# A ring of three load slots whose length becomes a multiple of 256 bytes

## The chip, the cores and the metric

The kernel runs on one core of a Trainium2 chip. A core has five engines with queues of their own: TensorE (PE in the profile, with its weight loads as PEld), VectorE (DVE), ScalarE (ACT), GpSimd (POOL) and SyncE (SP). Data comes from the memory outside the core through 16 DMA engines into the on-chip memory SBUF, which has 128 partitions; a tile here has a row of so many bytes in each partition. Matrix products are written into a second on-chip memory, PSUM.

The metric is the device time of one execution in microseconds (us), and the median over several executions is compared.

## The reference

Two attention blocks decode one token against a cache of 8192 positions, and a gate mixes their outputs. Everything is float32.

```python
# x: 1x1x448.  A: 16 heads with 16 key/value heads.  B: 16 heads with 8 key/value heads.  Dh = 256
q = (x @ wq).reshape(16, 256)
scores = q @ k_cache.T * 256 ** -0.5          # per head, 8192 positions
p = softmax(scores)
o = p @ v_cache                                # per head, 256
out = o.reshape(16 * 256) @ wo                 # 448
g = sigmoid((x * gate_w).sum())
result = g * out_A + (1 - g) * out_B           # both from the same x
```

The two caches make nearly all of the input: 24 key/value heads of 8192 x 256 numbers, for keys and for values, are 403 MB; with the projection matrices the core reads 432 MB, each byte once.

## The kernel before

**One stream.** The host lays all inputs end to end in one array, `stream`, in the order in which the kernel wants them. The function `plan()` makes that order. It goes over eight sets; a set is one key/value head of B (with two query heads) and two heads of A. Each head's keys and values are cut into four tiles of 128 partitions x 4096 numbers (`ROWS * DH`), and a value tile follows its key tile three tiles later (`LEAD`). Query weights (`wq`) come ahead of the set that they serve, output weights (`wo`) behind it.

**Fills.** `plan()` cuts the stream into 54 fills, `LOADS`, without regard to where a tile ends: a fill has 15872 numbers (`FULL`) for each partition, 63488 bytes, and the first has 8 numbers (`XG`) more, the input vector and the gate weights. Fills 0 to 50 are loaded by one DMA each. The last three are cut into smaller DMAs, 2, 3 and 7 of them. So 50 loads move 128 rows of 63488 bytes, and load 0 moves 128 rows of 63520 bytes. In the stream the rows of a load lie end to end.

**The ring.** Line 464 takes a buffer `buf`, named `slot`, from the pool `ring`, which has `SLOTS = 3` buffers and uses them in turn. The length of a buffer is `FULL + XG` = 15880 numbers, 63520 bytes of a partition, since the first fill needs that much. Line 468 issues the load on SyncE's queue, into the buffer from its first byte on (`c` is 0 at the start of each fill). SyncE waits there until the engines have read what the buffer held three fills before; this is what sets the order of loads against compute. The engines then wait for the load's semaphore.

The pools follow one another in a partition: `const` up to byte 8960, the ring from there, and the pool of working tiles, `small`, behind it. In the built program the three slots begin at bytes 8960, 72480 and 136000. Loads 0, 3, 6, ... go to 8960 (called slot A here), loads 1, 4, 7, ... to 136000 (slot C), and loads 2, 5, 8, ... to 72480 (slot B). The number 8960 is 35 x 256; 72480 is 32 past a multiple of 256, and 136000 is 64 past one.

**What the engines do with a slot.** `piece()` takes each part of a fill to its consumer. Keys of most heads are laid out transposed, and `scores()` multiplies them with the query on TensorE (line 255); VectorE takes the minimum of the negated scores (line 261), ScalarE the exponential (264), and VectorE transposes the result (267). For the first head of A in each set (`BY_ROW`), `scores_by_row()` does the product on VectorE: line 277 multiplies the key tile with the query in place, in the slot, and line 281 sums each position's 256 products. `attend()` multiplies the weights with the value tile on TensorE (line 307). Every fourth tile, a head is closed: `take`, `gather`, `combine`, `column` and `project_o` turn its sums into 256 numbers, and `emit_set` multiplies a set's heads with `wo` (line 380). The last set's output weights arrive last, and `emit` (line 397), a copy (line 482) and the store (line 483) end the program.

Of the kernel before, what the change touches and what calls it, by code (L numbers as in the profile page):

```python
# [7 lines left out]
F32 = mybir.dt.float32  # L8
# [6 lines left out]
P = 128  # L15
# [12 lines left out]
FULL = 15872  # L28
# [12 lines left out]


XG = 2 * (KF + 1)
ATOM = {"xg": XG, "k": 2 * DH, "v": 2 * DH, "wq": 2 * DH, "wo": D}


def plan():

    size = {"xg": XG, "k": ROWS * DH, "v": ROWS * DH, "wq": WQ, "wo": 8 * D}
    per = len(UNITS) * NT  # L50
# [15 lines left out]
    for kind, i in items[:items.index(last[0])]:  # L66
        at, left = 0, size[kind]
        while left:
            step = min(left, room) // ATOM[kind] * ATOM[kind]
            if step:  # L70
# [24 lines left out]
def kernel(  # L95
# [9 lines left out]
    ring = ctx.enter_context(tc.tile_pool(name="ring", bufs=SLOTS))  # L105
# [309 lines left out]
    def piece(kind, i, at, view):  # L415
        n = view.shape[-1] // ATOM[kind]
        j0 = at // ATOM[kind]
        if kind == "xg":
            inputs(view[:, :KF + 1])
            GW[0] = view[:, KF + 1:]  # L420
        elif kind == "wq":
            project(i, j0, view.rearrange("p (c n) -> p c n", c=n))
            if j0 + n < 2 * KF + 1:
                pass
            elif i == 0:
                spread(0)
                prepare(GW[0])
            else:
                wait(1, spread, i)
        elif kind == "k":  # L430
            u, t = TILES[i]
            if u in BY_ROW:
                scores_by_row(u, t, 2 * j0, view.rearrange("p (j d) -> p j d", d=DH))
            else:
                scores(u, t, j0, view.rearrange("p (c n) -> p c n", c=n))
            if j0 + n < 2 * NG:
                return
            tick()
            if t == NT - 1:
                gather(u)  # L440
                wait(1, combine, u)
                wait(2, column, u)
        elif kind == "v":
            u, t = TILES[i]
            n = view.shape[-1] // DH
            attend(u, t, at // DH, n, view.rearrange("p (j d) -> p j d", d=DH))
            if at // DH + n == ROWS:
                if t == NT - 1:
                    take(u)
                    if u != TILES[-1][0]:  # L450
                        wait(1, project_o, u)
                if i >= len(TILES) - LEAD:
                    tick()
        elif kind == "wo" and i < NS - 1:
            emit_set(i, j0, view.rearrange("p (c n) -> p c n", c=n))
            if i == NS - 2 and j0 + n == 8:
                fold()
        else:
            for j in range(n):
                LAST[divmod(j0 + j, 2)] = view[:, j * D:(j + 1) * D]  # L460

    off = 0
    for fill in LOADS:
        buf = ring.tile([P, FULL + XG], F32, name="slot")
        c = 0
        for load in fill:
            n = sum(x[3] for x in load)
            nc.sync.dma_start(buf[:, c:c + n], stream[off:off + P * n].rearrange("(p n) -> p n", p=P))
            off += P * n
            for x in load:  # L470
                piece(*x[:3], buf[:, c:c + x[3]])
                c += x[3]
# [78 lines left out]
```

## Time and profile before

| | us |
|---|---|
| median of 3 runs | 1010.08 |
| lowest and highest run | 1009.97, 1012.16 |
| span of the profiled execution, first to last instruction | 1008.4 |

The profiled execution's own time is known by its span alone; the rest of the 1010.08 us lies around the span, or is the difference of that execution to the median.

How to read the lines below. The page's first part gives for each engine its busy time, its share of the span and the number of its instructions. The second part cuts the span into 40 slices and gives busy tenths, for the DMA engines too. The third gives for a DMA queue the packets, the megabytes and the time of these packets as a share of 16 engines' time; asked for a stretch of time, the same view counts the packets that start in it, with their whole time, so in a short stretch the share can be over 100%. The fourth is the chain of work that ended last, followed back from the end; in its long form each row has a start, a length and a name, and a DMA's length goes from the issue to the landing. DMA issues are listed with their size and the time from issue to landing. In rows of waits stand the total, the number and the longest. `L281` is line 281 of the kernel.

### The profile page before, as it was taken

How to read it: one execution, taken by the hardware profiler on the slowest of the kernel's cores; microseconds unless marked ns; L12 is line 12 of the kernel's file. 1: busy time of each engine (PE TensorE's matmuls, PEld its weight loads, DVE VectorE, ACT ScalarE, POOL GpSimd, SP SyncE). 2: the span in 40 equal slices, each digit the busy share in tenths (PEclk: the TensorE clock that was granted, in tenths of full speed). 3: DMA queues.
4: the chain of work that ended last, by engine and by line, in shares of the span. 5: the costliest groups of instructions: out<-in, count | busy, mean ns of one | idle time of the engine just before them, and what ended most of it. 6: DMA issues, size and time to landing. Idle time of an engine off the chain costs nothing.

```text
span 1008.4 us, 7568 instructions
## 1 busy us (share of the span) xinstructions
PE 584.2 (58%) x3154; PEld 171.4 (17%) x3154; DVE 458.2 (45%) x644; ACT 92.8 (9%) x307; POOL 1.9 (0%) x10
## 2 busy tenths in 40 slices
PE   0855845664655555746646576655665637536567
PEld 0211211121111111212111121111211112111112
DVE  1386213961248521576214841248521585206851
ACT  0100100010100110001100000100110100101010
POOL 0000000000000000000000000000000000000000
PEclk9877787777787787877777767776787867877878
DMA  9999999999999999999999999999999999999997
GB/s 403 442 438 418 434 436 439 418 441 431 441 436 426 424 441 438 429 426 442 431 428 441 431 429 434 436 434 431 432 431 441 439 423 424 439 443 431 418 426 310
DMA packets 9113, 432.49 MB, mean 429 GB/s; under 512 B 1016, under 2 KB 1144, under 8 KB 1784
## 3 DMA queue, kind: packets, MB, share of 16 engines
q1 hardware_dynamic: 9080, 432.02, 99.2%
q8 instruction: 24, 0.39, 0.2%
q14 instruction: 9, 0.07, 0.0%
HBM read 432.02 MB, written 0.00 MB: 428 GB/s over the span
## 4 chain that ended last, share of the span: by engine, by line
DMA 72%; DVE 15%; PE 11%; ACT 1%; issue 1%; another core or an unknown queue 0%; SPq 0%; ACTq 0%; DVEq 0%
DMA slot<-in_stream_dram 72%; DVE sr L281 6%; DVE slot L277 6%; PE o L307 5%; PE sc L255 4%; PE sm L220 1%; ACT px L264 0%; DVE mn L261 0%; DVE pr L294 0%; ACT pxr L290 0%; DVE pr L267 0%; ACT ew L346 0%; DVE wr L353 0%; PE sm L371 0%; DVE mt L287 0%
## 5 line engine op out<-in xcount | busy, mean ns | idle before, releaser
L307 PE MATMUL o<-slot,pr 128*32 128x512 f32 (+1 forms) x1536 | 352.4, 764 | 220.2 <-DMA slot<-in_stream_dram 220.2
L255 PE MATMUL sc<-slot,qb 128*32 128x512 f32 x1024 | 199.0, 725 | 102.5 <-DMA slot<-in_stream_dram 102.3
L261 DVE TENSOR_REDUCE mn<-sc 128x1 f32<-128x512 f32 x64 | 44.1, 690 | 334.3 <-PE sc L255 311.5
L277 DVE TENSOR_TENSOR slot<-slot,qa 128x4096 f32<-128x4096 f32 (+7 forms) x40 | 142.6, 3565 | 43.6 <-DMA slot<-in_stream_dram 43.6
L307 PEld LDWEIGHTS o<-slot,pr 128*32 128x32 f32 (+1 forms) x1536 | 80.6, 143 | 403.5 <-DMA slot<-in_stream_dram 249.0
L281 DVE TENSOR_REDUCE sr<-slot 128x16 f32<-128x4096 f32 (+7 forms) x40 | 142.7, 3567 | 1.4
L255 PEld LDWEIGHTS sc<-slot,qb 128*32 128x32 f32 x1024 | 47.1, 132 | 221.2 <-issue 125.5
L264 ACT ACTIVATE px<-sc,st 128x512 f32<-128x512 f32 x64 | 44.0, 687 | 408.1 <-DVE st L262 366.5
L267 DVE STREAM_TRANSPOSE pr<-px 128x512 f32<-128x512 f32 x64 | 45.6, 713 | 59.5 <-ACT px L264 59.5
L220 PE MATMUL sm<-slot,xz 128*32 128x512 f32 x128 | 47.2, 717 | 36.8 <-DVE xz L193 22.9
L290 ACT ACTIVATE pxr<-sr,st 128x16 f32<-128x16 f32 x32 | 9.8, 308 | 372.9 <-DVE st L288 372.9
L371 PE MATMUL sm<-sel,ob 128*128 128x1 f32 (+1 forms) x96 | 18.2, 294 | 36.6 <-DVE ob L317 36.6
L317 DVE SCALAR_TENSOR_TENSOR ob<-o,half,ob 128x256 f32<-128x256 f32 x24 | 11.3, 473 | 43.6 <-ACT ob L316 43.6
L371 PEld LDWEIGHTS sm<-sel,ob 128*128 128x128 f32 x96 | 16.2, 237 | 60.5 <-DVE ob L317 54.9
L220 PEld LDWEIGHTS sm<-slot,xz 128*32 128x32 f32 x128 | 11.3, 129 | 67.0 <-issue 28.4
L294 DVE TENSOR_TENSOR pr<-pxr,cols 128x256 f32<-128x256 f32 x32 | 13.6, 426 | 15.9 <-ACT pxr L290 15.9
L237 PE MATMUL sm<-px,spread 64*128 64x256 f32 x16 | 7.1, 533 | 14.4 <-DVE es L347 14.4
L360 PE MATMUL sm<-ones,wr 1*128 1x1 f32 x48 | 9.6, 268 | 9.2 <-DVE wr L353 9.2
L316 ACT ACTIVATE ob<-o,half 128x256 f32<-128x256 f32 x24 | 11.3, 469 | 39.7 <-PE o L307 39.6
L380 PE MATMUL Y<-slot,ocs 128*1 128x448 f32 x112 | 14.1, 621 | 0.0
L360 PEld LDWEIGHTS sm<-ones,wr 1*128 1x128 f32 x48 | 7.8, 203 | 32.6 <-issue 32.6
L264 ACT ACTIVATION_READ_ACCUMULATOR px<-sc,st 128x1 f32 x64 | 12.3, 193 | 0.0
(73 smaller groups left out, 137.5 us busy)
## 6 DMA issues: line engine op xcount, KB each, us to landing
slot<-in_stream_dram SPq DMA_DIRECT2D x50, 7936.0 KB, 42.5
slot<-in_stream_dram SPq DMA_DIRECT2D x1, 7940.0 KB, 21.8
slot<-in_stream_dram SPq DMA_DIRECT2D x1, 4864.0 KB, 41.2
slot<-in_stream_dram SPq DMA_DIRECT2D x2, 2048.0 KB, 25.3
slot<-in_stream_dram SPq DMA_DIRECT2D x1, 3072.0 KB, 30.1
slot<-in_stream_dram SPq DMA_DIRECT2D x1, 1280.0 KB, 20.8
slot<-in_stream_dram SPq DMA_DIRECT2D x1, 1024.0 KB, 23.5
slot<-in_stream_dram SPq DMA_DIRECT2D x2, 512.0 KB, 24.8
```

Source lines behind the costliest of these rows:

```text
L220: nc.tensor.matmul(q[BLK * a:BLK * (a + 1), :], xz[:, c if c < KF else KF + a, :], w[:, j, :], start=(c == 0), stop=(c == KF), skip_group_ ...
L255: nc.tensor.matmul(sc[32 * g:32 * (g + 1), :], qb[:, e, at:at + 32], kt[:, j, :], start=(e == 0), stop=(e == 1), skip_group_check=True)
L261: nc.vector.tensor_reduce(mn, sc, axis=AX.X, op=OP.min)
L264: nc.scalar.activation(px, sc, AF.Exp, bias=st[:, 0, t:t + 1], scale=-1.0, accum_out=st[:, 1, t:t + 1])
L267: nc.vector.transpose(pr.rearrange("p (q r k) -> p q k r", r=BLK, k=2), px.rearrange("p (q k c) -> p q k c", c=BLK, k=2))
L277: nc.vector.tensor_tensor(kt, kt, QA[u][:, None, :].to_broadcast([P, n, DH]), op=OP.mult)
L281: nc.vector.tensor_reduce(sc[:, j0:j0 + n], kt, axis=AX.X, op=OP.add)
L294: nc.vector.tensor_tensor(pr, px[:, :, None, :].to_broadcast([P, ROWS // 2, NG * NT, 2]), cols[:, t].rearrange("p g r -> p (g r)")[:, None ...
L307: nc.tensor.matmul(O[u][w * g:w * (g + 1), :], pr[:, j // 2, :w], vt[:, j - j0:j - j0 + 2, :], start=(t == 0 and j < 2 * P // w), stop=(t ...
L360: nc.tensor.matmul(cl, WR.pop(u).rearrange("p c x m k -> p (c x m k)"), ones[:1, :], start=True, stop=True)
L371: nc.tensor.matmul(oc[:, e, :M], OB[u][:, e::2], SEL[u][:, :M], start=True, stop=True)
L380: nc.tensor.matmul(YY[0][32 * h:32 * h + 1, :], OC[s, r][:, e, m:m + 1], wt[:, j, :], start=False, stop=(s == NS - 2 and e == 1), skip_gro ...
```

## The change

A slot becomes 15936 numbers long in place of 15880, which is 63744 bytes of a partition, 249 x 256, in place of 63520. The three slots then begin at bytes 8960, 72704 and 136448, all multiples of 256, and the working tiles behind the ring begin at byte 200192 in place of 199520. What is loaded, in which order and into which slot in turn, stays; so do the sources in `stream`. The last 56 numbers of a slot are never written or read.

```diff
 XG = 2 * (KF + 1)
+SLOT = 15936
 ATOM = {"xg": XG, "k": 2 * DH, "v": 2 * DH, "wq": 2 * DH, "wo": D}
...
     for fill in LOADS:
-        buf = ring.tile([P, FULL + XG], F32, name="slot")
+        buf = ring.tile([P, SLOT], F32, name="slot")
         c = 0
```

## The prediction

> **What bounds the kernel now.** I read the page's first three parts, then the chain that ended last, then the DMA issues, and last the DMA view of single microseconds. The page first:
>
> ```profile
> span 1008.4 us, 7568 instructions
> PE 584.2 (58%) x3154; PEld 171.4 (17%) x3154; DVE 458.2 (45%) x644; ACT 92.8 (9%) x307; POOL 1.9 (0%) x10
> ...
> DMA  9999999999999999999999999999999999999997
> ...
> q1 hardware_dynamic: 9080, 432.02, 99.2%
> ...
> DMA 72%; DVE 15%; PE 11%; ACT 1%; issue 1%; another core or an unknown queue 0%; SPq 0%; ACTq 0%; DVEq 0%
> ```
>
> No engine is busy for 60% of the span, while the 16 DMA engines are busy in every slice and at 99.2% in all. The chain gives DVE 15% and PE 11%, and a reader could take those for work that the transfers wait for. They are not. The chain follows SyncE's issue of a load back to the engine that freed the slot, but when that issue comes the earlier loads are still streaming. Two rows of the DMA issues show it, the first load (issued at 0.74 us with nothing ahead of it), and the load issued at 214.24 us, the shortest landing that the view gives for any later full load:
>
> ```profile
> slot<-in_stream_dram SPq DMA_DIRECT2D x1, 7940.0 KB, 21.8
> slot<-in_stream_dram SPq DMA_DIRECT2D x1, 7936.0 KB, 34.7
> ```
>
> A load with free engines lands 21.8 us after its issue; the most hurried later one takes 34.7, so it stood 12.9 us in line. The transfers never ran dry: a slot could be freed up to 12.9 us later and no byte would be later. The bound is the pace of the transfers, and the chain in order of time tells it (start, length; start plus length is a landing):
>
> ```profile
> 81.06 36.75 DMA slot<-in_stream_dram
> ...
> 127.38 46.64 DMA slot<-in_stream_dram
> ...
> 192.92 37.30 DMA slot<-in_stream_dram
> ...
> 545.30 42.38 DMA slot<-in_stream_dram
> ...
> 607.34 36.54 DMA slot<-in_stream_dram
> ...
> 985.78 18.75 DMA slot<-in_stream_dram
> ...
> 1004.57 0.99 PE Y L397 x32
> ```
>
> Landings at 117.81, 174.02 and 230.22 us lie 56.21 and 56.20 apart, those at 587.68 and 643.88 again 56.20: each time three loads, one into each slot, so 18.73 us a load of 7936 KB, or 434 GB/s. The last landing is at 1004.53, and 3.9 us of tail follow. The span is 1008.4 and the median of the runs 1010.08, so 1.7 us lie around the span or between that execution and the median; I keep them.
>
> **The change part by part.** It has two effects. The first is where a load's rows begin. Slot A, for loads 0, 3, 6 and so on, begins at byte 8960 of a partition before and after, 35 times 256. Slot C, for loads 1, 4, 7, moves from 136000 (64 bytes past a multiple of 256) to 136448 (a multiple). Slot B, for loads 2, 5, 8, moves from 72480 (32 bytes past) to 72704. So the kernel before already holds the experiment: a third of its loads are aligned. What a misaligned row costs is the difference between the slots' row transfers. The DMA view over windows of 1.00 us that hold nothing but whole rows of 63488 bytes gives it; the last number is the time of these rows as a share of 16 engines' time in the window. First slot A (load 45, from 852.53 us), then C (load 46, from 871.24), then B (load 47, from 889.93):
>
> ```profile
> q1 hardware_dynamic: 15, 0.95, 219.6%
> ...
> q1 hardware_dynamic: 15, 0.95, 219.6%
> ...
> q1 hardware_dynamic: 15, 0.95, 220.1%
> ```
>
> 219.6% of 16 us over 15 rows is 2342.4 ns a row in slots A and C; 220.1% is 2347.7 ns in slot B. Being 64 bytes past costs nothing that shows; being 32 past costs 5.3 ns. Slot B earlier, load 5 from 100.38 us and load 20 from 383.38 us:
>
> ```profile
> q1 hardware_dynamic: 15, 0.95, 219.7%
> ...
> q1 hardware_dynamic: 14, 0.89, 205.4%
> ```
>
> These are 2343.5 and 2347.4 ns. So the extra is about 1 ns early and 5 ns from somewhere before load 20 on. A load is 128 rows, 8 for each of 16 engines (8 x 2342.4 ns is 18.74 us, the chain's 18.73). Slot B takes 17 whole loads (2, 5, ... 50). If all paid 5.3 ns, the change is worth 17 x 8 x 5.3 ns = 0.72 us. If loads 20 to 50 pay 5.3 and the six before pay 1.1, it is 8 x (11 x 5.3 + 6 x 1.1) ns = 0.52 us. The chain speaks for less: with 5.3 ns on one load of three, a late cycle should be 0.04 us longer than an early one, and 643.88 - 587.68 is 56.20, as early. The extra may lie within engines that aren't the last to land, and then it is worth nothing. The ends are 0.72 us and 0; I take 0.4, near their middle, since one kind of row supports each end. Slot C adds 0: its row reads as A's. Could an aligned row cost more than a misaligned one? The windows exclude it, since A's rows are nowhere above B's or C's.
>
> The Trainium skill, page "DMA: Bandwidth & Descriptors", section "How a descriptor splits into AXI transactions", says that a transfer that doesn't begin on a 256-byte boundary starts its first transaction at the boundary below and pays the skipped bytes in beats of 32 bytes. By it slot B would lose one beat a row and slot C two; at 1.18 ns a beat (2342.4 ns for 1984 of them) 17 x 8 x 3 x 1.18 ns makes 0.48 us, an estimate from that page, and the time would be 1009.6 us. The trace agrees in size and disagrees in which slot: C, with two beats to lose, loses none.
>
> The second effect is a shift of everything behind the ring. The working tiles (`px`, `pr`, `st` and the rest) begin at 200192 in place of 199520, and SyncE, TensorE, VectorE, ScalarE and GpSimd get the same instructions with the same waits in the same order; no DMA is added, split or moved past another. Engine operands in slots B and C shift too. No row shows the working tiles at another address, so I bound their cost by the slots, which three addresses do show. VectorE's two passes over a k tile:
>
> ```profile
> L281 DVE TENSOR_REDUCE sr<-slot x40: 686/4420/4422, 52.2 to 960.5; 128x16 f32<-128x4096 f32 x24, 128x4 f32<-128x1024 f32 x3, 128x12 f32<-128x3072 f32 x3, 128x10 f32<-128x2560 f32 x2
> ...
> L277 DVE TENSOR_TENSOR slot<-slot,qa 128x4096 f32<-128x4096 f32 x24 | 106.0, 4418 | 18.7 <-DMA slot<-in_stream_dram 18.7
> ```
>
> The full reduction has median 4420 and maximum 4422 ns over tiles in all three slots, so an offset of 32 or 64 bytes moves it by 2 ns or less. I cost the shift at zero. What hides it otherwise is the 12.9 us in line. In the tail it isn't covered: 3.9 us of small work after the last landing, of which even 5% would be 0.2 us, up or down.
>
> Sum, on the profiled span: 1008.4 - 0.4 + 0 = 1008.0, and on the median 1010.08 - 0.4 = 1009.7 us, which is 0.04% and less than a measurement of this kernel can tell from no change (about 0.2%, 2.0 us; its three runs went from 1009.97 to 1012.16).
>
> **The rivals.** *The change touches the transfers not at all.* The 5.3 ns may belong to the third place in the cycle and its neighbours in time, not to the address. Load 5's 1.1 ns at the same address and C's zero speak for it; that the extra is there in windows of loads 20 and 47 speaks against. Time 1010.1 us. The Trainium skill's page "SBUF — State Buffer", section "A bandwidth-pool intuition that's wrong (but worth ruling out)", would also have it so: HBM, at about 358 GB/s a core, is nearly always what limits, not SBUF. Here the rate is 434, so this run doesn't sit at that figure.
>
> *Faster by more than 0.2%.* Misalignment costs at each 256-byte piece of a row, not only at its head, so that both other slots gain. A row has 248 such pieces, and its 2342.4 ns come to 1.18 ns for 32 bytes; if each piece lost the time of 32 bytes, that would be 293 ns a row, 34 x 8 x 293 ns = 80 us in all, and 930 us. To reach 2.0 us, 7.4 ns a row in both slots are enough (34 x 8 x 7.4 ns). C's 0 and B's 5.3 say no; only a cost between rows, outside their recorded time, could hide it.
>
> *Slower by more than 0.2%.* With all three slots equal modulo 256, VectorE's passes over one slot and the writes into another begin at like offsets and get in each other's way. The place is the release of a slot by L281:
>
> ```profile
> SPq L468 <- DVE sr L281: 477.3, 24, 24.2
> ```
>
> A slot holds at most 3.9 tiles of 4096 and so at most 3.9 x (4418 + 4420) ns = 34.5 us of the two passes. The point of decision is 12.9 us more than that, 37%; at 50% a release would be 17.2 us later, 4.3 beyond the cover, and once in each of the eight sets that is 34 us, 1044. Against it: slot A and slot C sit 64 bytes apart already, and no pass in the span exceeds the median by more than 2 ns.
>
> **How the numbers follow.** The small gain (1009.7) gets 0.52, no effect (1010.1) 0.38, the faster rival 0.04, the slower one 0.03, and 0.03 goes to a median that lands 0.2% high by the spread of runs alone, as one of the three runs shown did. The first two are both within 0.2%: same 0.90, faster 0.04, slower 0.06. The range takes 0.72 us of gain and a further 0.7 for the runs below (1008.6), and above reaches into the spread of the runs shown, 1011.2, short of the highest.
>
> **What would show it.** Right: windows in loads of slot B read 219.6% for 15 rows, late in the span as well; cycles of three loads stay at 56.20 us; the DMA share stays at 99%; L281 keeps 4420 ns. The first rival shows if B keeps its 220.1% at its new address. The prediction is wrong if a cycle falls below 56.1 us, which only a cost between rows explains, or if a full load lands in about 22 us, which means that the line ran dry.

## The result and the profile after

| | before | changed |
|---|---|---|
| median | 1010.32 us (21 runs) | 1008.87 us (21 runs) |
| lowest, highest | 1009.83, 1012.16 | 1008.40, 1010.60 |
| ratio of the changed kernel to the one before | | 0.9986 (95% interval 0.9980 to 0.9991) |

The changed kernel is 1.45 us faster, with an interval of 0.9 to 2.0 us. That is 0.14%, in the forecast range and within the 0.2% that was called no change, but about three and a half times the 0.4 us that was forecast. The span varies less than the whole time: its median is 1008.2 us over the 93 runs of the kernel before that stood beside the experiments (1008.1, 1008.3 and 1008.2 in their three groups), and 1007.0 over the 21 runs of the changed one. So some 1.2 us of the 1.45 lie inside the span.

The page of the changed kernel has the same shape: span, engines, the DMA line and the first queue.

```profile
span 1007.7 us, 7568 instructions
PE 570.9 (57%) x3154; PEld 167.4 (17%) x3154; DVE 458.1 (45%) x644; ACT 92.7 (9%) x307; POOL 1.9 (0%) x10
...
DMA  9999999999999999999999999999999999999997
...
q1 hardware_dynamic: 9080, 432.02, 99.2%
```

The DMA share is 99.2% as before: the transfers are still the bound, and only their pace can have changed. The DMA view over a window of 1.00 us that holds nothing but rows of 63488 bytes, in load 45 (slot A, from 851.84 us), load 46 (C, from 870.56) and load 47 (B, from 888.62):

```profile
q1 hardware_dynamic: 11, 0.70, 161.0%
...
q1 hardware_dynamic: 11, 0.70, 161.0%
...
q1 hardware_dynamic: 10, 0.63, 146.4%
```

161.0% of 16 us over 11 rows and 146.4% over 10 are 2341.8 and 2342.4 ns, which is the same within the rounding of the share. Slot B's 2347.7 ns are gone; all three slots read alike. The chain in order of time shows what it did to the pace:

```profile
193.10 37.20 DMA slot<-in_stream_dram
...
237.92 48.51 DMA slot<-in_stream_dram
...
545.49 41.83 DMA slot<-in_stream_dram
...
604.25 39.21 DMA slot<-in_stream_dram
...
653.56 46.00 DMA slot<-in_stream_dram
...
984.88 18.49 DMA slot<-in_stream_dram
1003.41 1.45 PE Y L398 x32
```

Landings at 230.30 and 286.43 lie 56.13 us apart, those at 587.32, 643.46 and 699.56 lie 56.14 and 56.10 apart, where the kernel before had 56.20. These cycles of three loads are 0.06 to 0.10 us shorter. They are single ones; by the mean start of a load's 128 rows in the packet records, a cycle became 0.07 us shorter from load 17 to load 50 and 0.03 us from load 2 to load 17. The last landing came at 1003.37 in place of 1004.53, 1.16 us earlier. The spans of these two executions differ by 0.7 us only, since what follows the last landing took 4.3 us in place of 3.9. VectorE's sum over a tile is what it was, at a median of 4420 ns:

```profile
L282 DVE TENSOR_REDUCE sr<-slot x40: 686/4420/4421, 52.1 to 959.7; 128x16 f32<-128x4096 f32 x24, 128x4 f32<-128x1024 f32 x3, 128x12 f32<-128x3072 f32 x3, 128x10 f32<-128x2560 f32 x2
```

### The profile page after: what moved, and what is told of

It reads as the page before. It is cut to its first block, busy times and chain, and to the rows that moved or that the text cites. A ratio compares the mean times of both kernels' runs of the same rounds, so it can differ in the third digit from the quotient of the medians.

```text
span 1007.7 us, 7568 instructions
## 1 busy us (share of the span) xinstructions
PE 570.9 (57%) x3154; PEld 167.4 (17%) x3154; DVE 458.1 (45%) x644; ACT 92.7 (9%) x307; POOL 1.9 (0%) x10
## 3 DMA queue, kind: packets, MB, share of 16 engines
q1 hardware_dynamic: 9080, 432.02, 99.2%
## 4 chain that ended last, share of the span: by engine, by line
DMA 72%; DVE 15%; PE 11%; ACT 1%; issue 1%; another core or an unknown queue 0%; SPq 0%; ACTq 0%; DVEq 0%
DMA slot<-in_stream_dram 72%; DVE sr L282 6%; DVE slot L278 6%; PE o L308 5%; PE sc L256 4%; PE sm L221 1%; ACT px L265 0%; DVE mn L262 0%; DVE pr L295 0%; ACT pxr L291 0%; DVE pr L268 0%; ACT ew L347 0%; DVE wr L354 0%; PE sm L372 0%; DVE mt L288 0%
## 5 line engine op out<-in xcount | busy, mean ns | idle before, releaser
L308 PE MATMUL o<-slot,pr 128*32 128x512 f32 (+1 forms) x1536 | 342.6, 737 | 225.8 <-DMA slot<-in_stream_dram 225.8
L282 DVE TENSOR_REDUCE sr<-slot 128x16 f32<-128x4096 f32 (+7 forms) x40 | 142.7, 3567 | 1.4
## 6 DMA issues: line engine op xcount, KB each, us to landing
slot<-in_stream_dram SPq DMA_DIRECT2D x1, 7940.0 KB, 22.1
```

What stands on the lines that cost most here:

```text
L282: nc.vector.tensor_reduce(sc[:, j0:j0 + n], kt, axis=AX.X, op=OP.add)
L308: nc.tensor.matmul(O[u][w * g:w * (g + 1), :], pr[:, j // 2, :w], vt[:, j - j0:j - j0 + 2, :], start=(t == 0 and j < 2 * P // w), stop=(t ...
```

## The experiments

Each was timed in five rounds against the kernel before. The table at the end of this section gives, besides the times, the mean length of a row in each slot.

**All slots 32 past.** An unused tile ahead of the ring moves three equally spaced slots.

```diff
+    head = ctx.enter_context(tc.tile_pool(name="head", bufs=1))
     ring = ctx.enter_context(tc.tile_pool(name="ring", bufs=SLOTS))
...
+    spare = head.tile([P, 8], F32, name="spare")
+    nc.vector.memset(spare, 0.0)
...
-        buf = ring.tile([P, FULL + XG], F32, name="slot")
+        buf = ring.tile([P, 15936], F32, name="slot")
```

> Slots are 63744 bytes long as in the changed kernel, and an unused tile of 32 bytes stands ahead of the ring, so all three slots begin 32 bytes past a multiple of 256. Theory 1 (the address: a row that begins at an odd multiple of 32 bytes takes longer): every load pays what slot B paid before. Rows in windows of all three slots read about 2347 ns, and with the 1.45 us that 17 loads cost, 51 loads cost 4.3 us over the changed kernel, 1013.2 us; by 5.3 ns a row it is 2.2 us and 1011.1. Theory 2 (the third place in the cycle, with slots of unequal spacing): spacing is that of the changed kernel, so 1008.9 and rows at 2342 ns. Theory 3 (the beats skipped below a 256-byte boundary, one here): 1.18 ns a row, 0.5 us, 1009.4.

Measured: 1011.41 us, 1.0013 of the kernel before (1.0004 to 1.0022). Rows of loads 45 (slot A, from 853.43 us) and 47 (B, from 890.94):

```profile
q1 hardware_dynamic: 15, 0.95, 220.1%
...
q1 hardware_dynamic: 16, 1.02, 234.7%
```

These are 2347.7 and 2347.0 ns, in slot A too, which had been free. The time is near the 1011.1 us that the rows' price gave, and not the 1013.2 of three times the measured gain. The place in the cycle (theory 2, no cost) and the skipped beats (theory 3, 1.18 ns a row) fall. What stands is a cost of some 5.5 ns a row for an address 32 past, in any slot.

**All slots 64 past.** The same with a spare tile of 16 numbers; the lines show the difference to the kernel with 32.

```diff
-    spare = head.tile([P, 8], F32, name="spare")
+    spare = head.tile([P, 16], F32, name="spare")
```

> As the kernel before this one, with 64 unused bytes ahead of the ring: all three slots begin 64 bytes past a multiple of 256. Theory 1 (odd multiples of 32): 64 is free, rows at 2342 ns, 1008.9 us, as the changed kernel. Theory 3 (skipped beats, two here): 2.4 ns a row, rows at 2344.8 ns, 51 x 8 x 2.4 ns = 1.0 us more, 1009.9. If only multiples of 256 are free for another reason, about what the kernel with 32 bytes shows.

Measured: 1010.66 us, 1.0007 (0.9998 to 1.0015). Rows of loads 45 (from 852.81 us) and 46 (from 878.59):

```profile
q1 hardware_dynamic: 13, 0.83, 190.7%
...
q1 hardware_dynamic: 14, 0.89, 205.4%
```

2347.1 and 2347.4 ns; over the late loads, 17 to 50, the mean is 2346.6. So 64 past is not free, and theory 1, which took odd multiples of 32 alone for the cause, falls in this form. But then slot C of the kernel before, 64 past, should have paid, and in its windows it did not.

**The old ring, 32 further on.** The slots keep 63520 bytes, and the spare tile of 8 numbers stands ahead: A 32, C 96, B 64 past.

```diff
+    head = ctx.enter_context(tc.tile_pool(name="head", bufs=1))
     ring = ctx.enter_context(tc.tile_pool(name="ring", bufs=SLOTS))
...
+    spare = head.tile([P, 8], F32, name="spare")
+    nc.vector.memset(spare, 0.0)
```

> The slots keep the old length of 63520 bytes, and 32 unused bytes stand ahead of the ring: slot A begins 32, slot B 64 and slot C 96 bytes past a multiple of 256. Theory 1 (odd multiples of 32): loads of A and C pay and B, the one that paid before, doesn't; rows about 2347 ns in A and C and 2342 in B; 34 loads cost twice what 17 did, 1008.9 + 2.9 = 1011.8 us (1010.3 to 1011.8, as the rows or the medians price it). Theory 2 (third place in the cycle): B alone pays, 1010.3. Theory 3 (skipped beats 1, 2 and 3): all three pay, 2.0 x 1.18 ns a row on average, 1009.9.

Measured: 1010.71 us, 1.0006 (0.9997 to 1.0015). All three slots pay: means of 2347.4 (A, 32), 2346.4 (C, 96) and 2346.6 ns (B, 64). None of the three theories gives that: the skipped beats have all three pay, but 1.2, 3.5 and 2.4 ns, with C the dearest.

**Only the working tiles moved.** A gap of 672 bytes behind the old ring.

```diff
+    gap = ctx.enter_context(tc.tile_pool(name="gap", bufs=1))
...
+    spare = gap.tile([P, 168], F32, name="spare")
+    nc.vector.memset(spare, 0.0)
```

> The ring is that of the kernel before (slots of 63520 bytes, B 32 past a multiple of 256), and 672 unused bytes behind it put the working tiles at byte 200192, where the changed kernel has them. If the slots' address is the whole cause, 1010.3 us with B's rows at 2347 ns late in the span. If the place of the working tiles gave the part of the 1.45 us that the rows don't explain (0.7 us), 1009.6.

Measured: 1010.06 us, 1.0000 (0.9991 to 1.0008), with the row means of the kernel before to 0.1 ns. The interval reaches about 0.9 us to either side, and the median span, 1008.2 us, is that of the kernel before; so the place of the working tiles has no part in the gain that these runs can tell.

**C alone at 64.** From here on the slots are those of the changed kernel, and the load is written from a later byte of its slot. What is added to `c` counts numbers of 4 bytes. The line with `enumerate` stands in every kernel from here on except the one at 16, and isn't shown again.

```diff
-    for fill in LOADS:
+    for place, fill in enumerate(LOADS):
...
-        c = 0
+        c = (0, 16, 0)[place % 3]
```

> The slots of the changed kernel, all on multiples of 256, but loads 1, 4, 7, ... (slot C) are written from byte 64 of the slot, so C alone is 64 past, as it was in the kernel before, and A and B are aligned. In the kernel before, rows of C read 2342 ns, in the kernel with all slots at 64 they read 2346.6. If the offset itself costs (the kernel before hid it for some reason of its own), rows of C read 2346.6 and the time is 1008.9 + 17 x 8 x 4.6 ns = 1009.5 to 1009.8 us. If 64 is free in company of aligned slots and costs where its neighbours cost, rows of C read 2342 and the time is 1008.9.

Measured: 1008.80 us, 0.9986 (0.9977 to 0.9995): as fast as the changed kernel, with a third of its loads misaligned. Load 46 (slot C, from 877.23 us):

```profile
q1 hardware_dynamic: 11, 0.70, 161.0%
```

2341.8 ns, and 2342.1 over C's late loads. A misaligned load with two aligned ones ahead of it is free at 64.

**The two offsets exchanged.** C at 32, B at 64.

```diff
-        c = 0
+        c = (0, 8, 16)[place % 3]
```

> Aligned slots; loads of C are written from byte 32 and loads of B from byte 64, the two offsets of the kernel before with places exchanged. Theory of the address: C's rows read 2347.5 and B's 2346.6 or 2342; by the medians of the four runs so far 1010.0 to 1011. Theory of the place (what comes third in the cycle pays, if it isn't aligned): B's rows read 2346 to 2348, C's 2342, 1010.3. In both the sum of the rows' excess says the time: 1.4 us for each us that the mean row's excess makes in a DMA engine.

Measured: 1010.08 us, 0.9999 (0.9990 to 1.0008), the time of the kernel before. Load 46 (C, from 871.25 us) and load 47 (B, from 889.83):

```profile
q1 hardware_dynamic: 15, 0.95, 219.6%
...
q1 hardware_dynamic: 14, 0.89, 205.2%
```

2342.4 ns in C, and 2345.1 in B, with a mean of 2346.9 over B's late loads. It is again the second misaligned load of the two that pays most, and now that one is at 64. So it isn't the address alone; what came ahead counts. Within C the rows are not alike: with the 128 rows of load 25 in order of their start, sixteen at a time, the means are 2342.0, 2342.0, 2342.0, 2342.0, 2342.5, 2344.6, 2348.8 and 2347.7 ns. The last groups hold rows of the next load too, since the 16 engines aren't in step.

The records don't name the engine, but they let the rows be joined. A row starts 3 to 4 ns before the end of another one, and 2 to 3 ns after it where a new load begins; followed from end to start, the rows fall into 16 lines of work, one for an engine, with 8 rows a load. Where two engines end together a join can be mistaken. Joined so, the eight rows of an engine read, as means over the late loads, 2342.0 to 2342.3 ns in the first five of C and 2344.2, 2347.7 and 2347.8 in its last three; 2345.9 to 2347.4 in B; and in A, which is aligned, still 2345.4, 2343.7 and 2342.9 in the first three, then 2342.0. The price sets in within C and fades within A.

**All loads at 128, and at 16.** Two more offsets; the first pair of lines is the one at 128 bytes, the second the one at 16.

```diff
-        c = 0
+        c = (32, 32, 32)[place % 3]
...
-        c = 0
+        c = 4
```

> Aligned slots, every load written from byte 128 of its slot. Excess of a row so far: 5.4 ns at 32, 4.6 at 64, 4.5 at 96 (all loads unaligned). If it is a matter of 256 alone, rows at 128 cost about the same, 4.0 to 4.6 ns, and the time is 1010.5 to 1010.9. If 128 is a boundary of its own, rows read 2342 and the time is 1008.9. By skipped beats (four) it would be 4.7 ns at 128, but then 64 should have been 2.4 and 32 1.2.

> Aligned slots, every load written from byte 16 of its slot, so a row begins in the middle of a 32-byte piece, which neither kernel does. If only the head and tail of a row cost, rows read 2347 to 2350 ns and the time is 1011 to 1013. If every 32-byte piece of the row is touched twice, rows take up to twice as long and the time goes towards 2000; already one further 256-byte piece in ten (25 of 248, 9.4 ns each) would be 0.24 us a row and 1105 us.

Measured: 1010.76 us at 128, 1.0007 (0.9998 to 1.0016), and 1011.85 us at 16, 1.0018 (1.0010 to 1.0027). 128 isn't a boundary of its own. A row that begins in the middle of a 32-byte piece costs 6.6 ns, too little for a cost at each piece; it must lie at few places of the row, such as its head and tail. With all loads misaligned the prices are 6.6 ns at 16, 5.6 at 32, 4.6 at 64 and 4.3 at 128.

**Every other load at 32.**

```diff
-        c = 0
+        c = 8 * (place % 2)
```

> Aligned slots of 63744 bytes; even loads are written from byte 0 of the slot and odd loads from byte 32, so each of 25 whole misaligned loads stands between two aligned ones. So far a full load at 32 costs 2.55 us / 51 = 0.05 us (1011.4 against 1008.85). If every misaligned row pays, 25 loads cost 1.25 us: 1010.1. If a DMA engine has some 36 ns in hand that misaligned rows use up (5.4 ns each at 32) and aligned rows restore, the first six or seven of its eight rows in an odd load read 2342 ns and the rest 2347, some 8 ns a load: 0.2 us, 1009.0 to 1009.1.

Measured: 1009.78 us, 0.9995 (0.9986 to 1.0004), between the two forecasts; the median span is 1007.8, where every row's price would give 1008.3 (half of the way from 1007.0 to 1009.6). Load 45, misaligned, in its middle (from 852.13 us) and at its end (from 861.89):

```profile
q1 hardware_dynamic: 15, 0.95, 219.6%
...
q1 hardware_dynamic: 9, 0.57, 132.1%
```

2342.4 and 2348.4 ns: the same load begins free and ends paying. Joined by engine, the eight rows of a misaligned load read 2342.0, 2342.0, 2342.0, 2342.1, 2342.3, 2344.2, 2347.6 and 2347.6 ns, and the first three of the aligned load behind it 2347.3, 2343.5 and 2343.0. Over both, about half of what eight misaligned rows cost is paid: 16 rows at 1.4 ns make 22 ns of 8 x 5.6 = 45. So eight aligned rows save the rows around them some 22 ns, 2.8 ns each.

**Aligned up to load 24, then at 32, and at 224.** The first pair of lines is the one at 32 bytes, the second the one at 224.

```diff
-        c = 0
+        c = 8 if place >= 25 else 0
...
-        c = 0
+        c = 56 if place >= 25 else 0
```

> Aligned slots; loads 0 to 24 are written from byte 0, loads from 25 on from byte 32. Both readings of the price (each row, or what is left after 36 ns in hand) give nearly all of loads 26 to 50 at 2347.5 ns and 1008.85 + 25 x 0.05 = 1010.1 us. They differ in load 25: with something in hand most of its rows read 2342, the last ones 2347; with a price on each row all read 2347.

> As the kernel before this one, with byte 224 in place of 32, the last 32-byte place ahead of a boundary of 256. Rows with all loads misaligned read 6.4 ns over 2342 at 16, 5.4 at 32, 4.6 at 64, 4.5 at 96 and 4.3 at 128, so perhaps 2 to 4 at 224, and 1009.3 to 1009.9 us. With something in hand (36 ns) a cheaper row lasts longer: 9 to 18 rows of an engine, so load 25 is free and load 26 begins free too. If instead a load pays because the load ahead of it was misaligned, load 26 pays whole from its first rows, as load 25 of the kernel with 32 is free whole.

Measured: 1010.29 us at 32, 1.0002 (0.9993 to 1.0010), and 1010.46 at 224, 1.0001 (0.9993 to 1.0010). With the step to 32, loads 25 (from 474.68 us), 27 (from 514.45) and 29 (from 549.59):

```profile
q1 hardware_dynamic: 12, 0.76, 175.7%
...
q1 hardware_dynamic: 11, 0.70, 161.1%
...
q1 hardware_dynamic: 10, 0.63, 146.8%
```

2342.7, 2343.3 and 2348.8 ns. The means over whole loads are 2342.3 in load 25, then 2342.9, 2343.6, 2346.4, 2347.4 and 2347.5. They rise over four loads, so "a load pays because the one ahead was misaligned" falls, and so does a price that each row pays at once. Something is used up. Its size, 36 ns by my reckoning from a single aligned load, is too small for this case: at 5.5 ns a row and 8 rows a load, loads 25 to 28 leave 42, 37, 31 and 9 ns unpaid, 119 ns together on the mean of the engines, after 25 aligned loads.

Joined by engine, the rise is a mixture: each engine goes from 2342 ns to the full price within a row or two, at a row of its own. Each engine also pauses now and then between two rows, for 0.3 us or about 1 us. Nine engines pay from rows 3 to 6 of load 28 on, after 26 to 29 free rows (143 to 160 ns at 5.5 ns each). Two that had last paused in loads 21 and 19 pay after 17 and 23 rows, two that paused in load 24 after 3 and 5, and three that pause in loads 26, 27 and 28 pay from the next row on. So what is used up belongs to each engine, a pause empties it, and aligned rows fill it: 26 aligned rows since the pause are worth 17 free rows, 94 ns, and 43 are worth 23, 127 ns, some 3 to 4 ns an aligned row, where the kernel with every other load at 32 gave 2.8. The step to 224 reads the same within 0.3 ns, load by load, and shows the same picture by engine, so 224 is as dear as 32, though I had guessed 2 to 4 ns.

The table: bytes past a multiple of 256 in slots A, C and B; mean row in loads 17 to 50, in ns, from the packet records of each trace, sorted by start, 128 to a load, rows over 2400 ns (31 to 49 in a trace) left out; median span and median time in us.

| kernel | A, C, B | row A | row C | row B | span | time |
|---|---|---|---|---|---|---|
| before | 0, 64, 32 | 2343.0 | 2343.0 | 2347.5 | 1008.2 | 1010.32 |
| only the working tiles moved | 0, 64, 32 | 2343.0 | 2343.0 | 2347.5 | 1008.2 | 1010.06 |
| changed | 0, 0, 0 | 2342.0 | 2342.0 | 2342.0 | 1007.0 | 1008.87 |
| C alone at 64 | 0, 64, 0 | 2342.0 | 2342.1 | 2342.1 | 1007.0 | 1008.80 |
| exchanged | 0, 32, 64 | 2342.8 | 2343.7 | 2346.9 | 1008.1 | 1010.08 |
| every other load at 32 | 0 or 32 | 2343.4 | 2343.4 | 2343.4 | 1007.8 | 1009.78 |
| all at 128 | 128 | 2346.2 | 2346.3 | 2346.4 | 1008.8 | 1010.76 |
| all at 64 | 64 | 2346.6 | 2346.6 | 2346.7 | 1008.9 | 1010.66 |
| old ring 32 further on | 32, 96, 64 | 2347.4 | 2346.4 | 2346.6 | 1008.9 | 1010.71 |
| all at 32 | 32 | 2347.6 | 2347.6 | 2347.7 | 1009.6 | 1011.41 |
| all at 16 | 16 | 2348.6 | 2348.6 | 2348.7 | 1010.1 | 1011.85 |

The rows carry most of the time. A kernel's mean row above 2342.0 ns, times the 408 rows that an engine moves in loads 0 to 50, gives its span above the changed kernel's within 0.4 us: 5.6 ns make 2.3 us for all at 32 (measured 2.6), 4.6 make 1.9 for all at 64 (1.9), 6.6 make 2.7 for all at 16 (3.1), 2.5 make 1.0 for the kernel before (1.2). This takes the late rows' price for the early loads too, and it is too much for them: summed as recorded, all rows of loads 0 to 50 give 1.94, 1.49, 2.40 and 0.76 us. Loads 0 to 2 read 2343 to 2346 ns in every kernel, the changed one too.

What aligned rows give back explains which mixtures pay. With the 2.8 ns an aligned row from the kernel with every other load at 32, a cycle of the kernel before should pay 8 x 5.6 + 8 x 4.6 - 8 x 2.8 = 59 ns, 2.5 ns a row, and the exchanged one the same; by the table both pay 2.5. With C alone at 64, 16 aligned rows give back 45 ns, more than the 37 of C's rows, and nothing is left to pay; by the table it is 0.1. No run was made to test this sum; it is fitted on one kernel and holds for three others.

## Why the prediction was right, and where it was short

*The bound.* Right. The first load of the changed kernel lands 22.1 us after its issue, and the shortest landing that the view gives for any later full load, issued at 214.42 us, takes 34.6:

```profile
slot<-in_stream_dram SPq DMA_DIRECT2D x1, 7940.0 KB, 22.1
...
slot<-in_stream_dram SPq DMA_DIRECT2D x1, 7936.0 KB, 34.6
```

So it stood 12.5 us in line; the transfers didn't run dry, and the time followed the rows.

*The price of slot B.* Right as a rate: B read 2347.7 ns and now reads 2342.4. Of the two sums made from it, the smaller one, 0.52 us with six cheap early loads, was near: from load 12 on, where the rows of the changed kernel have settled, B's recorded rows lost 0.55 us, and the loads ahead next to nothing (0.04 us over all slots). That the range held the result is in part luck: 0.72 us of gain below 1010.08 ends at 1009.4, and 1008.87 lies within the further 0.7 us that was left for the spread of the runs.

*Taking 0.4 us, the middle between 0.72 and 0.* This is the step that failed, as a mis-sized term. The end at zero came from the chain: a late cycle of 56.20 us was no longer than an early one. That comparison could not price the rows. Loads 12 to 14 of the kernel before paid already (2342.6, 2342.6 and 2345.1 ns, 34 ns for the cycle), so only some 0.03 us could tell it from a late cycle with 60 ns, too little for single landings. The right yardstick was a cycle without misaligned rows, and it was not in the trace of before: it is 56.10 to 56.14 us, so these cycles of the kernel before held 0.06 to 0.10 us. The sign "cycles of three loads stay at 56.20" did not come.

*Slot C adds 0, slot A adds 0.* Right in mid-load, where the windows lay, and short over the whole load. Joined by engine, the last three rows of C read 2342.7, 2344.8 and 2346.6 ns and the first three of A 2347.4, 2343.8 and 2342.9. Rows of A and C were so 1.0 ns over 2342.0 on the mean of the late loads, and from load 12 on they lost 0.20 us. With B's 0.55 the rows give 0.75 us.

*A cost between rows.* The prediction gave it no term. The 17 long pauses of the engines between rows from load 12 on took 0.98 to 1.08 us in the kernel before and 0.86 to 0.95 in the changed one, with about one for each engine: all pauses together make 0.14 us an engine. With the rows that is 0.9 us of the 1.2 in the span. The rest, and the 0.25 us from 1.2 to 1.45, isn't assigned to anything; the interval of 0.9 to 2.0 takes it in.

*That C's zero meant that 64 bytes past costs nothing.* Wrong as a reading, though the term was near here. At 64 a row costs 4.6 ns where its neighbours are misaligned too; C's first rows were free because an aligned load came ahead of them. The rule of the Trainium skill, page "DMA: Bandwidth & Descriptors", section "How a descriptor splits into AXI transactions", has transactions start on multiples of 256 bytes. The runs agree on that boundary: of 16, 32, 64, 128 and 224 none was free once the loads around had it too, and all three aligned slots were free. By its skipped beats 64 should cost twice as much as 32 and 128 four times. The section speaks of bytes that are fetched; for these writes the prices don't follow it and fall, from 5.6 to 4.6 and 4.3 ns.

*The shift of the working tiles costs nothing.* Right as far as the runs can tell: 1.0000 with that shift alone (0.9991 to 1.0008), and L282 kept its 4420 ns.

*The rivals.* "No effect on the transfers" fell with all slots at 32: slot A, moved, paid. The sign it was given, slot B keeping 220.1%, did not come. The faster rival, a cost at each 256-byte piece, fell with the row at 16, which costs 6.6 ns and not hundreds. The slower rival, VectorE and writes in each other's way, had no sign at all in the median of L282.

## What to carry to other kernels

When a kernel is bound by its transfers, look for a place in its own trace where the suspected cost is absent, and measure against that; here aligned and misaligned slots stood side by side, and a 1 us window of the DMA view resolved one part in a thousand. Rounding a buffer's length so that each row starts on a multiple of 256 bytes costs a few hundred bytes and is worth doing, but with rows of 63488 bytes it is worth 0.14% here, and 0.3% against a kernel with all loads at 16. A slot that looks free of a cost may be living on what its neighbours leave it, so change the neighbours before calling it free.

## What the runs showed that was not expected

Misaligned rows don't pay at once. After 25 aligned loads a DMA engine that hadn't paused lately moved 26 to 29 rows at 32 past before the full 5.5 ns a row showed, 119 ns unpaid on the mean of all engines, and where aligned and misaligned loads alternate about half of the cost is paid. What aligned rows build up and misaligned rows use up goes by each engine's own rows since its last pause, while the other engines go on as they were; that speaks for something kept in each engine's path, and against the engines' places relative to each other. This is read from joined records and not from a run made for it, and what it is that is kept these runs don't show.

The price seems to go by the distance to the nearer multiple of 256, not by the bytes skipped below: 32 and 224, the one pair tried on both sides, cost the same within 0.3 ns, and it falls from 6.6 ns at 16 to 4.3 at 128.
